# Soft-MoE chain on one core: more weight pieces held early, the second experts' first weights split earlier, one direct block instead of two

## The chip, the core and the metric

The kernel runs on one core of one Trainium2 chip. A core has a matrix engine (TensorE, PE in the profile, with its weight loads shown apart as PEld), three engines for elementwise work (VectorE = DVE, ScalarE = ACT, GpSimd = POOL) and SyncE (SP), which issues the transfers between HBM and the core's memory here. The metric is the device time of one execution in microseconds, the median of several. A smaller number is better.

## The reference

Three steps follow one another: causal attention with decay, a soft mixture of experts over slots, and a dense mixture of experts. Cut to what is computed:

```python
# attention: batch 4, heads 8, S = 576, D = 64
scores = q @ k.T / 8 + (cum_i - cum_j), causal     # cum: running sum of log(clip(f))
x = softmax(scores) @ v                            # -> x: 2304 tokens x 512

# soft MoE: 8 experts, 4 slots each, F = 1024
logits = x @ phi                                   # 2304 x 32
slot_in = softmax(logits, axis=tokens).T @ x       # 32 x 512
slot_out[e] = relu(slot_in[e] @ w1[e]) @ w2[e]     # 4 x 512 per expert
x = softmax(logits, axis=slots) @ slot_out         # 2304 x 512

# dense MoE: 4 experts, F = 1024, every token
p = domain_probs / (sum + 1e-9)
out = sum_e p[:, e] * (relu(x @ m1[e]) @ m2[e])
```

Below, w1 and w2 are the weights of the eight slot experts, and m1 and m2 those of the four dense experts.

## The kernel before

**Stages.** (a) Attention, pair of heads by pair of heads, up to about 212 us. (b) Its end, with the last softmax over the slots (212 to 222 us; the code from L540 to L645). (c) The eight slot experts (222 to 257 us): per expert `layer1` (32 matmuls, ReLU on ACT into `hr`), `turn` (two transposes of `hr`, a copy on DVE into `ht`) and `layer2` (16 matmuls, summed in `so_ps`). The last expert's second layer, `layer2_last`, is done in two halves of columns, and DVE adds each half to `orow0` and `orow1`. (d) A transition (257 to 265 us): the combine weights are transposed (`c4_tr`, copied by `c4_hi` on ACT into `c4t`), `g_make` multiplies the slots' outputs with m1 of dense expert 0 (so the first dense layer costs 32 rows of slots and not 2304 tokens), `g_spread` lays that out as `gs`. (e) The four dense experts, nine blocks of 256 tokens each, 36 blocks (265 to 673 us).

**A block of stage (e).** `pieces` (8 matmuls, `c4t` times `gs`) writes the hidden layer of a block into the PSUM tiles `two0` and `two1`, four matmuls for each. ACT and DVE take the ReLU out as two rounded parts, a hi part and a lo part (`q`, `a`, `s` in the rows). The second layer, hidden times m2, is done with operands of the type fp32r as hi times hi, hi times lo and lo times hi. A **direct** block (L1043 in the rows, `d`) does it with 96 matmuls of 128x256. A **Strassen** block (L1023, `R`, `P`, `Q`) has seven products of 12 matmuls, 84 in all, and DVE must make sums of hidden pieces for it (`S1` to `S4`, L893), POOL their lo parts (L901). In both kinds DVE takes the results out of PSUM, scaled by p, into `acc` (`take`, L1004 and L1006). There are four PSUM banks for results, used in turn: a new one cannot be begun before DVE has taken out the one that held the bank.

**Weights of stage (e).** m2 of an expert is a 512x512 grid of four parts, B00, B10, B01, B11. Each needs a hi part (`w_hi`, a cast, `wh_B` in the rows) and a lo part (`w_lo`, source minus hi, L722, `wl_B`). Strassen products need B00, B10, B11 and four sums of parts, T1 to T4, made by POOL (`w_sum`, L703) and split the same way (`wh_T`, `wl_T`). For dense expert 0, m2 arrives last of all early weights, B's are split in the transition and in block 0, and T's in blocks 0 and 1 (table `PRE0`). Blocks 0 and 1 are direct (`ND = 2`), the others Strassen.

**Weights' way in.** SP streams pieces of 512 KB in the order of `stream`: w1, w2 of the slot experts, then m1, m2 of the dense ones. In attention 4 pieces go to the tile `ring` and `NB = 29` to the pool `ringb`, one every third step; more go to freed memory (`raw`, `opd`, `post`, `post2`) and, during the slot experts, to freed ring slots (table `later`). The m2 of dense expert 0 goes into `ring` last, behind the code of slot expert 5.

**What sets the order.** From attention on, a scheduler orders what is not fixed. In a region `manual_schedule(engines=...)` the named engines run in the order in which the code stands. In the transition these are PE, ACT and DVE, in the blocks also POOL; an instruction on an engine runs only when all before it on that engine are done. `busy(n)` puts n 128x128 matmuls of the identity on PE whose result nobody reads; a matmul on f32 data shows as two in the rows.

Of the kernel before, what the change touches and what calls it, by code (L numbers as in the profile page):

```python
# [34 lines left out]
def soft_moe_kernel(tc, a, out):  # L35
# [10 lines left out]
    NB = 29  # L46
    ND = 2
    with ExitStack() as top:
# [871 lines left out]
        with tc.manual_schedule(engines={E.PE, E.Activation, E.DVE}):  # L920
            turn(E1 - 2)
            layer1(E1 - 1)
            layer2(E1 - 2)
            turn(E1 - 1)
            c4_tr(B, c4_bank(B))
            c4_tr(0, c4_bank(0))
            for h in range(2):
                act.copy(orow[h], so_ps[:, 256 * h:256 * h + 256])
            free += [0, 1, 2, 3]
            c4_hi(B)  # L930
            c4_hi(0)
            for h in range(2):
                layer2_last(h)
            c4_rep(2)
            c4_tr(1, c4_bank(1))
            c4_hi(1)
            c4_rep(3)
            t = bank(0, 0)[:, 0:128].rearrange("p (c s) -> p c s", c=DC)
            for c in range(DC):
                pe.matmul(t[:, c, :], lhsT=orow[c // 2][:, c % 2 * 128:c % 2 * 128 + 128], rhs=i4)  # L940
            dve.tensor_copy(so_t, t)
            c4_tr(2, c4_bank(2))
            c4_hi(2)
            w_hi(0, "B00", act, 0, 2)
            w_lo(0, "B00", pool, 0, 2)
            w_hi(0, "B00", act, 2, 4)
            gg = g_make(0, bank(0, 1)[:, 0:256])
            c4_tr(3, c4_bank(3))
            c4_hi(3)
            cq.close()  # L950
            attn.close()
            accp = top.enter_context(tc.tile_pool(name="accp", bufs=1))
            wsp.append(top.enter_context(tc.tile_pool(name="wspb", bufs=1)))
            top.enter_context(tc.tile_pool(name="skew", bufs=1)).tile([128, 24], F32, name="skew")
            hp = top.enter_context(tc.tile_pool(name="hp", bufs=1))
            ttp = top.enter_context(tc.tile_pool(name="ttp", bufs=1))
            free += [4, 5, 6, 7]
            for hf in range(2):
                g_spread(0, *gg, hf)
            pieces(0, 0)  # L960
            hi_d(0, 0, 0)
            lo_d(0, 0, 0)
            w_hi(0, "B10", act, 0, 2)
            w_lo(0, "B10", pool, 0, 2)
            hi_d(0, 0, 1)
            lo_d(0, 0, 1)
            pieces(0, 1)
            hi_d(0, 1, 0)
            lo_d(0, 1, 0)
            w_lo(0, "B00", dve, 2, 4)  # L970
            w_hi(0, "B10", act, 2, 4)
            w_lo(0, "B10", pool, 2, 4)
            hi_d(0, 1, 1)
            lo_d(0, 1, 1)
            w_hi(0, "B01", act, 0, 2)
            w_lo(0, "B01", pool, 0, 2)
            w_hi(0, "B01", act, 2, 4)
            w_lo(0, "B01", dve, 2, 4)
            w_hi(0, "B11", act, 0, 2)
            w_lo(0, "B11", pool, 0, 2)  # L980
            w_hi(0, "B11", act, 2, 4)
            w_lo(0, "B11", dve, 2, 4)
            dve.tensor_reduce(dps, dpr, axis=AX.X, op=ALU.add)
            dve.tensor_scalar(dps, dps, 1e-9, None, op0=ALU.add)
            dve.reciprocal(dps, dps)
            dve.tensor_tensor(dpn, dpr, dps[:, :, None].to_broadcast([128, 18, E2]), op=ALU.mult)
# [246 lines left out]
```

## Time and profile before

| | us |
|---|---|
| median of 3 runs (lowest to highest) | 675.01 (674.58 to 676.32) |
| the profiled execution | 675.4 |
| its span, first to last instruction | 673.6 |
| PE busy in the span | 657.5 (98%) |
| DVE, POOL, ACT busy | 494.5 (73%), 419.0 (62%), 341.8 (51%) |
| slot experts, 220 to 255 us: PE busy, share of the DMA engines | 33.9 of 35, 0.95 |
| blocks 0 and 1 of the dense experts (265.05 to 290.36) | 25.3 |
| mean granted clock of PE | 0.99 of full speed |

Times in rows are microseconds from the start of the span, and 1.8 us of the execution lie around the span. PE is busy almost throughout, so what changes the time is what PE has to do and where it waits. "Busy" of a matmul row reaches to its modelled end, so matmul rows overlap the next one's start; the pace is read from starts.

### The profile page before, as it was taken

Reading aid. Unit: us, or ns where it says so; the run is one execution under the profiler, and the core shown is the slowest. Engines: PE = TensorE matmul, PEld = TensorE weight load, DVE = VectorE, ACT = ScalarE, POOL = GpSimd, SP = SyncE. Lnnn points to the kernel's source line nnn. Section 1 sums busy time; section 2 is a strip of 40 time slices with the busy share of each in tenths; the row PEclk is TensorE's granted clock in tenths of the full one; section 3 lists DMA queues with packets and bytes.
Section 4 is the critical chain, followed back from the end, with each engine's and each line's share of the span. In section 5 each row is a group of like instructions: output and inputs, shape, how many; then the busy total and the mean of one; then the engine's idle time right before and its main releaser. Section 6 shows DMA issues by size and latency. Waiting matters only on the chain.

```text
span 673.6 us, 15304 instructions
## 1 busy us (share of the span) xinstructions
PE 657.5 (98%) x5642; PEld 580.3 (86%) x5642; DVE 494.5 (73%) x1358; ACT 341.8 (51%) x817; POOL 419.0 (62%) x392
## 2 busy tenths in 40 slices
PE   5999999999999998999999999999999999999997
PEld 3877777777777446999999999999999999999997
DVE  7888988988986103976778876778876778877774
ACT  4776767767763015543446443446543356543441
POOL 5677767767751046944589844589934589935442
PEclk7999999999999999999999999999999999999999
DMA  6678788733318894033000303000303000011111
GB/s 184 189 261 254 220 279 262 229 93 117 93 55 310 334 419 165 2 126 126 1 1 2 126 1 125 2 1 2 124 3 111 15 1 1 32 37 59 48 48 63
DMA packets 27138, 76.15 MB, mean 113 GB/s; under 512 B 3772, under 2 KB 4156, under 8 KB 27064
## 3 DMA queue, kind: packets, MB, share of 16 engines
q1 hardware_dynamic: 27064, 75.18, 32.5%
q8 instruction: 45, 0.74, 0.5%
q14 instruction: 29, 0.24, 0.1%
HBM read 70.31 MB, written 4.72 MB: 111 GB/s over the span
## 4 chain that ended last, share of the span: by engine, by line
PE 91%; DVE 3%; ACT 2%; issue 2%; SPq 1%; DMA 1%; POOL 0%; ACTq 0%; DVEq 0%
PE R L1023 27%; PE Q L1023 13%; PE P L1023 6%; PE avb L276 6%; PE pt L258 5%; PE two L835 5%; PE sc L228 3%; PE d L1043 3%; PE sc L212 3%; PE sc L227 3%; PE two L731 2%; PE pl L324 2%; PE pt L249 2%; PE ava L288 2%; PE so_ps L755 2%
## 5 line engine op out<-in xcount | busy, mean ns | idle before, releaser
L901 POOL TENSOR_TENSOR s<-S,s 128x512 fp32r<-128x512 f32 x136 | 174.9, 1320 | 134.7 <-ACT s L897 134.7
L897 ACT CAST s<-S 128x512 fp32r<-128x512 f32 x136 | 75.0, 619 | 85.9 <-DVE S L893 47.9
L202 ACT ACTIVATE p<-p,nm 128x256 f32<-128x256 f32 (+2 forms) x144 | 83.4, 580 | 37.7 <-DVE nm L198 36.9
L1023 PE MATMUL R<-wh_T,s 128*128 128x256 f32 x544 | 86.6, 281 | 0.7 <-DVE acc L1006 0.7
L1006 DVE SCALAR_TENSOR_TENSOR acc<-R,dpn,acc 128x256 f32<-128x256 f32 x115 | 55.4, 482 | 37.2 <-PE R L1023 34.2
L867 ACT ACTIVATE a<-two 128x256 f32<-128x256 f32 x68 | 26.1, 384 | 96.9 <-PE two L835 90.5
L1023 PEld LDWEIGHTS R<-wh_T,s 128*128 128x128 f32 x544 | 73.4, 188 | 1.4 <-ACT a L876 1.2
L198 DVE CUSTOM_DVE_ANT_0 p<-sc,maskb 128x256 f32<-128x256 f32 (+2 forms) x144 | 66.1, 488 | 3.3 <-PE sc L212 0.9
L893 DVE SCALAR_TENSOR_TENSOR S<-two,S 128x256 f32<-128x256 f32 x136 | 57.0, 419 | 3.4 <-POOL s L901 0.8
L893 DVE SCALAR_TENSOR_TENSOR S<-two,a 128x256 f32<-128x256 f32 x136 | 56.2, 413 | 0.0
L179 POOL TENSOR_TENSOR opd<-raw,opd 64x576 fp32r<-64x576 f32 x30 | 44.6, 1487 | 11.2 <-ACT opd L168 9.8
L258 PE MATMUL pt<-ident,p 128*128 128x128 f32 x288 | 47.3, 283 | 1.8 <-DVE ptb L255 0.8
L227 PE MATMUL sc<-opd 128*128 128x256 f32 (+3 forms) x128 | 47.1, 378 | 1.6 <-ACT opd L168 1.6
L190 POOL TENSOR_TENSOR opd<-raw,opd 64x576 fp32r<-64x576 f32 x31 | 44.1, 1424 | 6.7 <-DVE opd L170 5.7
L258 PEld LDWEIGHTS pt<-ident,p 128*128 128x128 f32 x288 | 31.3, 142 | 17.6 <-issue 13.1
L835 PE MATMUL two<-c4t,gs 128*128 128x256 f32 x288 | 46.1, 283 | 0.3 <-ACT gs L168 0.3
L883 DVE SCALAR_TENSOR_TENSOR q<-two,q 128x512 fp32r<-128x512 f32 x68 | 46.2, 679 | 0.0
L1023 PE MATMUL R<-wh_T,q 128*128 128x256 f32 x272 | 43.8, 283 | 0.0
L276 PE MATMUL avb<-ptb,v 128*64 128x192 f32 (+3 forms) x384 | 43.8, 347 | 0.0
L1023 PE MATMUL Q<-wh_B,s 128*128 128x256 f32 x272 | 43.2, 281 | 0.0
L1023 PE MATMUL Q<-wh_T,s 128*128 128x256 f32 x272 | 43.1, 280 | 0.0
L1023 PE MATMUL R<-wh_B,a 128*128 128x256 f32 x272 | 43.0, 280 | 0.0
(244 smaller groups left out, 1662.5 us busy)
## 6 DMA issues: line engine op xcount, KB each, us to landing
w<-in_w SPq DMA_DIRECT2D x50, 512.0 KB, 4.9
ring<-in_m SPq DMA_DIRECT2D x28, 512.0 KB, 6.2
raw<-in_k SPq DMA_DIRECT2D x64, 144.0 KB, 2.8
v<-in_v SPq DMA_DIRECT2D x16, 320.0 KB, 4.0
out<-acc SPq DMA_DIRECT2D x18, 256.0 KB, 2.0
...
```

What stands on the lines that cost most here:

```text
L198: dve.tensor_tensor_reduce(out=pt_in[j][:, k0:k0 + n], in0=sc, in1=maskb[:, m0:m0 + n], scale=-SCALE, scalar=nm, op0=ALU.add, op1=ALU.min, ...
L202: act.activation(p, p, AF.Exp, bias=nm, scale=-1.0, accum_out=sums)
L227: pe.matmul(o, lhsT=qa[hh][:, qs], rhs=ka[hh][:, 0:n], start=True, stop=False)
L258: pe.transpose(t[:, i, :], pt_in[j][:, 128 * i:128 * i + 128], ident)
L276: pe.matmul(t[64 * hh:64 * hh + 64, q0:q1], lhsT=v_raw[pr][:kk, i, 64 * hh:64 * hh + 64], rhs=ptb[2 * pr + hh][:kk, b0:b0 + q1 - q0], star ...
L835: pe.matmul(t[:, j, k], lhsT=gs[e][:, 128 * fc:128 * fc + 128], rhs=c4t[:, nb * BLK:nb * BLK + BLK])
L883: dve.scalar_tensor_tensor(o[:, 1], i, 0.0, f32(o[:, 0]), op0=ALU.max, op1=ALU.subtract)
L893: dve.scalar_tensor_tensor(sv[m, name][:, c], half[m, h][:, :, k, 128 * t:128 * t + 128], 0.0, other, op0=ALU.max, op1=op)
L897: act.copy(tile_of(m, name)[:, 0], sv[m, name])
L901: (eng or pool).tensor_tensor(o[:, 1], sv[m, name], f32(o[:, 0]), op=ALU.subtract)
L1006: dve.scalar_tensor_tensor(o, t, pcol, o, op0=ALU.mult, op1=ALU.add)
L1023: pe.matmul(t, lhsT=a[:, c, :], rhs=w[:, c, :], start=first and x == 0 and c == 0, stop=x == 2 and c == 3, skip_group_check=True)
```

## The change

It does seven things.

1. `NB` 29 to 33: `ringb` has four more slots, and four more pieces are loaded in attention (every third step, and now at steps 48 and 96 too).
2. In `stream`, m2 of dense expert 0 is moved forward, and goes to `ring` after slot expert 0, not after 5.
3. `busy(3)` is added at the end of attention, and four matmuls of the identity after `c4_tr(3)`.
4. The splits of B00, B10 and B01 are moved into slot experts 6 and 7: hi on ACT, lo on DVE, each 128x1024 in one instruction. B11 hi follows in the transition, B11 lo in block 0.
5. POOL's order is now written out from slot expert 6 on (before, from block 0 on). POOL makes T1, T2 before `g_spread`'s place, T3, T4 after it.
6. `ND` 2 to 1: only block 0 is direct. The table `PRE0` puts the sums and splits of the T's earlier, since block 1 needs them.
7. `dynamic_dma_scratch_size` is 256 and not the default, which moves the addresses of tiles on one side of the memory by 16128 bytes.

The rest of the diff is a change of indentation. Cut to its core:

```diff
-    NB = 29
-    ND = 2
+    NB = 33
+    ND = 1
...
+        at = NB + 19
+        stream = stream[:at] + stream[8 * E1 + 4:8 * E1 + 8] + stream[at:8 * E1 + 4] + stream[8 * E1 + 8:]
...
-                if pre and g >= GW and g % PS == PO:
+                if pre and g >= GW and (g % PS == PO or g % 48 == 0):
...
             dnat(B - 1)
+            busy(3)
...
-        later = {0: (ring, 4), 1: (ringb, 8), 2: (ringb, len(stream) - 44), 3: (ringb, 4), 5: (ring, 4)}
+        later = {0: (ringb, 8), 1: (ringb, 8)}
...
+            if e == 0:
+                raws[0] = load_ring()
             if e in later:
-                if later[e][0] is ring:
-                    raws[0] = load_ring()
-                else:
-                    load_w(*later[e])
+                load_w(*later[e])
...
-        with tc.manual_schedule(engines={E.PE, E.Activation, E.DVE}):
...
+        top.enter_context(tc.manual_schedule(engines={E.PE, E.Activation, E.DVE, E.Pool}))
+        free += [0, 1, 2, 3]
+        turn(E1 - 2)
+        w_hi(0, "B00", act)
+        w_hi(0, "B10", act)
+        w_lo(0, "B00", dve)
+        layer1(E1 - 1)
+        layer2(E1 - 2)
+        w_hi(0, "B01", act)
+        turn(E1 - 1)
+        w_lo(0, "B10", dve)
+        w_lo(0, "B01", dve)
+        c4_tr(B, c4_bank(B))
...
         c4_tr(3, c4_bank(3))
         c4_hi(3)
+        for _ in range(4):
+            pe.matmul(bank(1, 1)[:, 0:128], lhsT=ident, rhs=ident)
...
+        for name in ("T1", "T2"):
+            for c0 in (0, 2):
+                w_sum(0, name, c0, c0 + 2)
         for hf in range(2):
             g_spread(0, *gg, hf)
         pieces(0, 0)
         hi_d(0, 0, 0)
         lo_d(0, 0, 0)
...
+        w_lo(0, "B11", dve)
...
-                (1, 0): [("hi", "T1", "a", 0, 4), ("lo", "T2", "d", 0, 4)],
-                (1, 1): [("lo", "T1", "p", 0, 4), ("hi", "T3", "a", 0, 4)],
...
+        PRE0 = {(0, 0): [("sum", "T3", 0, 2), ("sum", "T3", 2, 4), ("hi", "T1", "a", 0, 4)],
+                (0, 1): [("lo", "T1", "d", 0, 2)],
...
-    nc = bacc.Bacc("TRN2", target_bir_lowering=False, num_devices=1)
+    nc = bacc.Bacc("TRN2", target_bir_lowering=False, num_devices=1, dynamic_dma_scratch_size=256)
```

What the edits do to the order on the engines, at three places. In these rows a name ends in a number of its own, `ring_28`, `ring_44` are the tile with m2, `wh_0_B00` and `wl_0_B00` the hi and lo part of B00 of dense expert 0, and `two0`, `two1` the PSUM tiles.

DVE around slot experts 6 and 7, before:

```order
L746 COPY ht_7_3593<-two0_3240 128x8x4
L767 TENSOR_TENSOR orow0_3556<-orow0_3556,two1_3241 128x256
L767 TENSOR_TENSOR orow1_3557<-orow1_3557,two1_3241 128x256
L941 COPY so_t_3520<-two0_3240 128x128
L911 CAST gh_0_3676<-two0_3240 128x256
L912 TENSOR_TENSOR gl_0_3677<-two0_3240,gh_0_3676 128x256
L170 CAST gs_0_3680<-two1_3241 128x512
```

DVE at the same place, now:

```order
L749 COPY ht_6_3569<-two0_3252 128x8x4
L725 TENSOR_TENSOR wl_0_B00_3573<-ring_44_3328,wh_0_B00_3572 128x1024
L749 COPY ht_7_3610<-two0_3252 128x8x4
L725 TENSOR_TENSOR wl_0_B10_3576<-ring_44_3328,wh_0_B10_3575 128x1024
L725 TENSOR_TENSOR wl_0_B01_3606<-ring_44_3328,wh_0_B01_3605 128x1024
L770 TENSOR_TENSOR orow0_3563<-orow0_3563,two1_3253 128x256
L770 TENSOR_TENSOR orow1_3564<-orow1_3564,two1_3253 128x256
L949 COPY so_t_3527<-two0_3252 128x128
```

Three subtractions of 128x1024 now stand between the copies `ht_6`, `ht_7` and the two additions to `orow`, which PE needs for the slots' outputs.

DVE from the last lo part of block 0's hidden layer to the first results of block 0 (`acc0`, `acc1`), before; `q1_1`, `q2_1` are the hidden layer of block 1:

```order
L846 SCALAR_TENSOR_TENSOR q2_0_3727<-two1_3241,q2_0_3727 128x512
L722 TENSOR_TENSOR wl_0_B01_3742<-ring_28_3505,wh_0_B01_3741 128x512
L722 TENSOR_TENSOR wl_0_B11_3748<-ring_28_3505,wh_0_B11_3747 128x512
L983 TENSOR_REDUCE dps_3524<-dpr_3523 128x18
L846 SCALAR_TENSOR_TENSOR q1_1_3831<-two0_3240,q1_1_3831 128x512
L984 TENSOR_SCALAR dps_3524<-dps_3524 128x18
L985 RECIPROCAL dps_3524<-dps_3524 128x18
L986 TENSOR_TENSOR dpn_3521<-dpr_3523,dps_3524 128x72
L846 SCALAR_TENSOR_TENSOR q2_1_3834<-two0_3240,q2_1_3834 128x512
L1004 TENSOR_SCALAR acc0_3758<-d_0_0_0_3778,dpn_3521 128x256
L1004 TENSOR_SCALAR acc1_3759<-d_0_0_1_3779,dpn_3521 128x256
```

DVE at the same place, now, behind the last lo part of block 0's hidden layer, `w_lo` of B11 (128x1024) and the first of the small ones; `S1_1` to `S4_1` and `a11_1` are operands of the Strassen products of block 1:

```order
L983 TENSOR_SCALAR dps_3531<-dps_3531 128x18
L984 RECIPROCAL dps_3531<-dps_3531 128x18
L985 TENSOR_TENSOR dpn_3528<-dpr_3530,dps_3531 128x72
L725 TENSOR_TENSOR wl_0_T1_3805<-T1_0_3726,wh_0_T1_3804 128x512
L895 SCALAR_TENSOR_TENSOR S1_1_3846<-two0_3252,a21_1_0_3825 128x256
L895 SCALAR_TENSOR_TENSOR S2_1_3848<-two0_3252,S1_1_3846 128x256
L725 TENSOR_TENSOR wl_0_T1_3805<-T1_0_3726,wh_0_T1_3804 128x512
L885 SCALAR_TENSOR_TENSOR a11_1_3827<-two0_3252,a11_1_3827 128x256
L895 SCALAR_TENSOR_TENSOR S3_1_3875<-two0_3252,a21_1_0_3825 128x256
L895 SCALAR_TENSOR_TENSOR S4_1_3877<-two0_3252,S2_1_3848 128x256
L725 TENSOR_TENSOR wl_0_T2_3853<-T2_0_3729,wh_0_T2_3852 128x512
L1003 TENSOR_SCALAR acc0_3766<-d_0_0_0_3784,dpn_3528 128x256
```

Between the last lo part of block 0's hidden layer and the first result there were two weight splits, four small ones (`dps`, `dpn`) and two lo parts; now there are four weight splits (B11, twice T1, T2), the four small ones, and five operands of block 1.

POOL after the last combine weights (`c4_3`), before:

```order
L703 TENSOR_TENSOR T1_0_3796<-ring_28_3505 128x512
L722 TENSOR_TENSOR wl_0_B00_3656<-ring_28_3505,wh_0_B00_3655 128x512
L703 TENSOR_TENSOR T1_0_3796<-ring_28_3505 128x512
L722 TENSOR_TENSOR wl_0_B10_3724<-ring_28_3505,wh_0_B10_3723 128x512 x2
L722 TENSOR_TENSOR wl_0_B01_3742<-ring_28_3505,wh_0_B01_3741 128x512
L703 TENSOR_TENSOR ring_28_3505<-ring_28_3505 128x2x256
L722 TENSOR_TENSOR wl_0_B11_3748<-ring_28_3505,wh_0_B11_3747 128x512
L703 TENSOR_TENSOR ring_28_3505<-ring_28_3505 128x2x256
L703 TENSOR_TENSOR T2_0_3877<-T1_0_3796,ring_28_3505 128x512 x2
L703 TENSOR_TENSOR ring_28_3505<-ring_28_3505,T2_0_3877 128x2x256 x2
```

POOL at the same place, now:

```order
L706 TENSOR_TENSOR T1_0_3726<-ring_44_3328 128x512 x2
L706 TENSOR_TENSOR T2_0_3729<-T1_0_3726,ring_44_3328 128x512 x2
L706 TENSOR_TENSOR ring_44_3328<-ring_44_3328 128x2x256 x2
L706 TENSOR_TENSOR ring_44_3328<-ring_44_3328,T2_0_3729 128x2x256 x2
L725 TENSOR_TENSOR wl_0_T2_3853<-T2_0_3729,wh_0_T2_3852 128x512
L725 TENSOR_TENSOR wl_0_T3_3902<-ring_44_3328,wh_0_T3_3901 128x512
L903 TENSOR_TENSOR s0_1_3937<-S2_1_3848,s0_1_3937 128x512
L903 TENSOR_TENSOR s0_1_3937<-S1_1_3846,s0_1_3937 128x512
```

POOL's splits of B's are gone, and the eight sums run one behind the other, followed by half of the lo parts of T2 and T3 and then the lo parts of block 1's operands (`s0_1`), which in the kernel before only block 2 has.

## Rows read from the trace of the kernel before

**Rows 1.** The page's part 1: busy time, share of the span, instructions of each engine.
```profile
PE 657.5 (98%) x5642; PEld 580.3 (86%) x5642; DVE 494.5 (73%) x1358; ACT 341.8 (51%) x817; POOL 419.0 (62%) x392
```

**Rows 2.** What PE waited for: us in total, times, longest.
```profile
PE two L765 <- DVE orow L767: 0.6, 1, 0.6
...
PE two L820 <- DVE gl L912: 0.4, 1, 0.4
...
PE sa_e L614 <- DVE dnn L397: 0.4, 1, 0.4
...
PE d L1043 <- DVE wl_B L722: 0.2, 1, 0.2
```

**Rows 3.** Windows: us, each engine's busy time (instructions), granted clock, DMA share, GB/s.
```profile
220.00:255.00 35.00, 33.91 (x430) 15.69 (x426) 2.70 (x12) 4.83 (x13) 9.98 (x29) 1.00 0.95 378
...
268.00:290.00 22.00, 21.77 (x186) 21.57 (x185) 19.87 (x31) 12.49 (x23) 20.12 (x13) 1.00 0.08 27
```

**Rows 4.** PE's timeline: start, us, line, tiles, shapes, count [idle before].
```profile
216.55 1.16 PE L540 MATMUL busy<-ident 128*128 128x128 f32 x8
...
217.64 0.47 PE L395 MATMUL dn<-ident,dt_e 32*128 32x32 f32 x5
...
256.34 1.07 PE L765 MATMUL two<-w,ht 128*32 128x256 f32 x16 [0.61 <-DVE orow L767]
...
265.05 0.39 PE L1043 MATMUL d<-wh_B,q 128*128 128x256 f32 x1 [0.17 <-ACT q L842]
...
290.36 0.63 PE L1023 MATMUL R<-wh_B,a 128*128 128x256 f32 x4
```

**Rows 5.** DVE's timeline, slot expert 7 to block 1, same columns.
```profile
254.21 0.19 DVE L746 COPY ht<-two 128x32 f32<-128x32 f32 x1 [3.87 <-PE ct L673]
...
255.86 0.42 DVE L767 TENSOR_TENSOR orow<-orow,two 128x256 f32<-128x256 f32 x1 [1.46 <-PE two L765]
...
269.20 0.68 DVE L846 SCALAR_TENSOR_TENSOR q<-two,q 128x512 fp32r<-128x512 f32 x1
...
272.58 0.22 DVE L983 TENSOR_REDUCE dps<-dpr 128x18 f32<-128x72 f32 x1
...
274.18 0.97 DVE L986 TENSOR_TENSOR dpn<-dpr,dps 128x72 f32<-128x72 f32 x1
...
279.19 1.97 DVE L722 TENSOR_TENSOR wl_T<-T,wh_T 128x1024 fp32r<-128x1024 f32 x1
...
281.87 2.65 DVE L722 TENSOR_TENSOR wl_T<-ring,wh_T 128x1024 fp32r<-128x1024 f32 x1
```

**Rows 6.** POOL's timeline, transition to block 1.
```profile
261.87 1.29 POOL L703 TENSOR_TENSOR T<-ring 128x512 f32<-128x512 f32 x1 [2.61 <-issue]
...
277.52 2.56 POOL L703 TENSOR_TENSOR ring<-ring,T 128x512 f32<-128x512 f32 x2
...
280.04 3.40 POOL L722 TENSOR_TENSOR wl_T<-T,wh_T 128x1024 fp32r<-128x1024 f32 x1
...
283.38 3.40 POOL L722 TENSOR_TENSOR wl_T<-ring,wh_T 128x1024 fp32r<-128x1024 f32 x1
```

**Rows 7.** The weight splits on DVE by source: duration in ns, min/median/max.
```profile
L722 DVE TENSOR_TENSOR wl_T<-ring,wh_T x10: 678/682/2648, 281.9 to 581.5; 128x512 fp32r<-128x512 f32 x9, 128x1024 fp32r<-128x1024 f32 x1
```

**Rows 8.** The chain that ended last, in order of time: one product of 12 matmuls.
```profile
293.81 1.41 PE R L1023 x12
```

**Rows 9.** Groups by line and shape: busy us, mean ns of one, idle before.
```profile
L716 ACT CAST wh_B<-ring 128x1024 fp32r<-128x1024 f32 x9 | 9.4, 1049 | 0.0
...
L893 DVE SCALAR_TENSOR_TENSOR S<-two,a 128x256 f32<-128x256 f32 x136 | 56.2, 413 | 0.0
...
L883 DVE SCALAR_TENSOR_TENSOR a<-two,a 128x256 fp32r<-128x256 f32 x68 | 28.1, 414 | 0.0
...
L1004 DVE TENSOR_SCALAR acc<-d,dpn 128x256 f32<-128x256 f32 x8 | 3.5, 474 | 1.6 <-PE d L1043 1.6
```

**Rows 10.** SP's timeline: the four transfers of m2 of dense expert 0.
```profile
247.78 3.05 SPq L71 DMA_DIRECT2D ring<-in_m  x4
```

More of the change, by code (lines that the diff above doesn't have):

```diff
@@ L839, in hi_d @@
                 ss[m, k] = (hp.tile([128, 2, 4, 256], F32R, tag="q2", bufs=2, name=f"q2_{m}") if k else
-                            hp.tile([128, 2, 4, 256], F32R, tag=f"s{m % 2}", name=f"q1_{m}"))
+                            hp.tile([128, 2, 4, 256], F32R, tag="s1", name=f"q1_{m}"))
             o = ss[m, k][:, 0, 2 * h:2 * h + 2][:, js]
@@ L918, in c4_bank @@
             return ops.tile([128, DM], F32, tag="o", name=f"ct_{b}")
-        with tc.manual_schedule(engines={E.PE, E.Activation, E.DVE}):
[L921 to L986, printed above, removed]
@@ new lines, in soft_moe_kernel @@
+        top.enter_context(tc.manual_schedule(engines={E.PE, E.Activation, E.DVE, E.Pool}))
[11 more added lines that the diff above has]
+        c4_tr(B, c4_bank(B))
+        c4_tr(0, c4_bank(0))
+        for h in range(2):
+            act.copy(orow[h], so_ps[:, 256 * h:256 * h + 256])
@@ new lines, in soft_moe_kernel @@
+        c4_hi(B)
+        c4_hi(0)
+        for h in range(2):
+            layer2_last(h)
+        c4_rep(2)
+        c4_tr(1, c4_bank(1))
+        c4_hi(1)
+        c4_rep(3)
+        t = bank(0, 0)[:, 0:128].rearrange("p (c s) -> p c s", c=DC)
+        for c in range(DC):
+            pe.matmul(t[:, c, :], lhsT=orow[c // 2][:, c % 2 * 128:c % 2 * 128 + 128], rhs=i4)
+        dve.tensor_copy(so_t, t)
+        c4_tr(2, c4_bank(2))
+        c4_hi(2)
+        w_hi(0, "B11", act)
+        gg = g_make(0, bank(0, 1)[:, 0:256])
@@ new lines, in soft_moe_kernel @@
+        c4_tr(3, c4_bank(3))
+        c4_hi(3)
+        for _ in range(4):
+            pe.matmul(bank(1, 1)[:, 0:128], lhsT=ident, rhs=ident)
+        cq.close()
+        attn.close()
+        accp = top.enter_context(tc.tile_pool(name="accp", bufs=1))
+        wsp.append(top.enter_context(tc.tile_pool(name="wspb", bufs=1)))
+        top.enter_context(tc.tile_pool(name="skew", bufs=1)).tile([128, 24], F32, name="skew")
+        hp = top.enter_context(tc.tile_pool(name="hp", bufs=1))
+        ttp = top.enter_context(tc.tile_pool(name="ttp", bufs=1))
@@ new lines, in soft_moe_kernel @@
+        free += [4, 5, 6, 7]
+        for name in ("T1", "T2"):
+            for c0 in (0, 2):
+                w_sum(0, name, c0, c0 + 2)
+        for hf in range(2):
+            g_spread(0, *gg, hf)
+        pieces(0, 0)
+        hi_d(0, 0, 0)
+        lo_d(0, 0, 0)
+        hi_d(0, 0, 1)
+        lo_d(0, 0, 1)
+        pieces(0, 1)
+        hi_d(0, 1, 0)
+        lo_d(0, 1, 0)
+        hi_d(0, 1, 1)
+        lo_d(0, 1, 1)
+        w_lo(0, "B11", dve)
+        dve.tensor_reduce(dps, dpr, axis=AX.X, op=ALU.add)
@@ L987, in soft_moe_kernel @@
+        dve.tensor_scalar(dps, dps, 1e-9, None, op0=ALU.add)
+        dve.reciprocal(dps, dps)
+        dve.tensor_tensor(dpn, dpr, dps[:, :, None].to_broadcast([128, 18, E2]), op=ALU.mult)
         acc = [accp.tile([128, DM], F32, name=f"acc{i}") for i in range(18)]
```

168 lines of the change are left out of this document (83 added, 85 removed), and 7 rows, old and new, of the table PRE0.

## The prediction

> **What bounds the kernel now.** I read the busy shares first: PE is busy for 657.5 of 673.6 us [rows 1], so the time is what PE has to do, plus its few waits. The PE's own waits come next, and only four of them lie near the change: 0.6 us for `orow`, 0.4 for `gl`, 0.4 for `dnn` and 0.2 for a weight's lo part [rows 2]. The windows say that neither stage which the change touches starves PE. The slot experts keep PE busy for 33.91 of 35 us though the DMA engines are 0.95 busy, and blocks 0 and 1 keep it busy for 21.77 of 22 us. In that second window, however, DVE is busy for 19.87 and POOL for 20.12 of 22 us [rows 3]. That is what the reader should keep in mind: there is no room on DVE and POOL in just the stretch into which the change puts more of their work. PE's granted clock is 1.00 in both windows, so the clock gives nothing back there.
>
> The numbers below are made against the profiled execution, 675.4 us with a span of 673.6; the median of the runs is 675.0, so a sum of +x means 675.0 + x for the median.
>
> **Transfers (edits 1, 2, 7): 0.** PE is busy throughout attention, and the four more transfers there are issued by SP, which does no arithmetic. During the slot experts four pieces fewer are asked for, but PE had only 1.1 us of idle time there, little of it for weights. m2 of dense expert 0, which SP issued at 247.78 before [rows 10], now goes into the queue about 25 us sooner. It must: its first cast now runs at about 250. At 378 GB/s a piece of 0.52 MB takes 1.4 us, and some 13 pieces stand before its end from 222 on, so it is there at about 240. With 10 us to spare I take 0, with 0 to +0.5 as bounds. The moved addresses have no row; I take 0.
>
> **`busy(3)` (edit 3): +0.3.** A filler matmul on f32 data makes two rows; eight rows take from 216.55 to 217.64, 0.136 us each [rows 4]. Six are 0.8 us. They stand where PE waited 0.4 us for `dnn` [rows 2], so 0.4 is left, less about 0.1 for the overlap of a row with the next. Range 0.2 to 0.4.
>
> **Four fillers after `c4_tr(3)`: +0.55.** Eight rows of 0.136 are 1.1 us, in place of the 0.4 us for which PE waited for `gl` [rows 2]; 0.1 overlaps. If `gl` comes later by more than that, they are free, but the next paragraph moves PE and DVE alike, so I keep 0.45 to 0.65.
>
> **Splits in the slot experts (edit 4): +1.0.** On ACT the three casts of 1.05 us [rows 9] fit between the ReLUs of experts 6 and 7. On DVE, idle there, lo B00 fits before the copy `ht_7`. Lo B10 and lo B01 do not: they stand behind `ht_7` and ahead of the `orow` additions. `ht_7` ends at 254.40 [rows 5]. A 128x512 split takes 0.68 when nothing disturbs it [rows 7], so one of 128x1024 takes about 1.2 to 1.3, and two end at about 256.8, where the first `orow` addition used to begin at 255.86 [rows 5]. PE's second half of `layer2_last`, which began at 256.34 after its wait [rows 4], waits for that addition: +1.0. Bounds: 0.5 if the copy `ht_7` is released 0.4 earlier (it waited for a `ct` transposition behind the one it needs), 1.7 if POOL's operations on `c4_2` come between.
>
> **One direct block less, no lo waits (edits 4 and 6): -2.3.** From the first direct matmul to the first of block 2 there are 25.31 us [rows 4]. Twelve matmuls take 1.41 [rows 8], 0.117 each. The new pair is 96 + 84 matmuls of the second layer and 16 of `pieces`, 196 x 0.117 = 23.0 us, if PE waits for nothing. That is 1.4 for twelve matmuls fewer and 0.9 for waits on lo parts of B's, which are now made before.
>
> **DVE's new queue in blocks 0 and 1 (edits 4, 5, 6): +3.3.** This is the term that decides. I count from block 0's first matmul.
>
> PE needs 12.2 us for block 0 (96 matmuls and 8 of `pieces`, of 0.117). Block 1's first product then needs the bank of block 0's first result, so `take` must be past. DVE ends the last lo part of block 0's hidden layer at +4.0 (before at 269.88 [rows 5], +4.8, with a weight split of its own between). Behind it stand, in order: lo B11 1.2; the four small ones, which take 1.9 from 272.58 to 275.15 less one lo part of 0.68 [rows 5]; half of lo T1 0.68; S1, S2 0.83; half of lo T1 0.68; `a_lo` 0.41; S3, S4 0.83; half of lo T2 0.68; the take 0.47 [rows 7, 9]. That is 7.7, less 0.8 since each starts some 0.07 before the end of the one ahead. To this come the waits for POOL, worked out in the next paragraph, 1.8. The take is done at 4.0 + 7.7 - 0.8 + 1.8 = 12.7: PE waits 0.5 there. Then DVE has a second take 0.47, a lo part 0.68 (block 2's `pieces` wait for it), S1 to S4 1.65, `a_lo` 0.41, two takes 0.95, a lo part 0.68, half of lo T3 0.68 with 0.7 of waiting, and the take of block 1's first product 0.48: 6.0 net of overlaps, so 18.7. PE's third product adds into that very bank, and undisturbed it is due after 104 + 24 + 4 = 132 matmuls, at 15.4. So PE is late by 3.3 in all, in three or four waits of 0.3 to 1.5 each. Behind it the chain is shorter than PE's work, and I expect nothing more.
>
> The waits for POOL come from a pair of rows. A lo T of 128x1024 on DVE started at 279.19 while POOL's sums ran until 280.08, and took 1.97, where two of 0.68 would be 1.3. POOL's split, begun at 280.04, took 3.40, where two of 1.28 are 2.56; DVE's next, begun at 281.87 in that split, took 2.65 and ended 1.1 after it [rows 5, 6]. So a subtraction on DVE with both inputs in SBUF and one on POOL seem to run one after the other, never together. In block 0 POOL has eight sums and two halves of lo parts of 1.28 each in a row, from about the end of `g_make` until +10. Each two-input operation on DVE meets one that is half through on the mean, 0.6: lo B11, one half of T1, and 0.6 more on the small ones than in their rows: 1.8. Bounds: without any such exclusion the term is +0.3, and with a full POOL operation of waiting each time +5.
>
> The Trainium skill says the same in "SBUF — State Buffer", section "Who interferes with whom": a DVE instruction with two SBUF inputs contends with a POOL instruction that reads SBUF, and the one that comes second blocks fully. By that rule the term is the +3.3; if the rows had another cause it would be +0.3. The trace agrees with the rule [rows 5, 6].
>
> **Sum.** 0 + 0.3 + 0.55 + 1.0 - 2.3 + 3.3 = +2.9: 678.3 for the profiled execution, 677.9 for the median.
>
> **Rivals.** What a measurement of this kernel can tell from no change is about 0.3%, 2.0 us, so "same" is 673.0 to 677.0.
>
> *DVE keeps up (not slower).* If the rows of 1.97 and 2.65 us owe their length to something other than the exclusion, DVE has 4.0 + 7.7 - 0.8 = 10.9 at the first take, before the 12.2 at which PE asks for it. That is the point which decides: 1.3 us of waits for POOL. The last term becomes +0.3 or less, the sum 0.3 + 0.55 + 1.0 - 2.3 + 0.3 = -0.15, 674.9; the favourable bounds (0.2, 0.45, 0.5, 0) give -1.15, 673.9. With half of the waits it is near 676. For it: DVE waits are worked out, not seen, and POOL's order could leave DVE first. Against it: three rows fit the exclusion to 0.1 us.
>
> *Faster.* Were the fillers and the splits in front of `orow` to cost nothing as well, -2.3 would stand alone, 672.7. Against it: a filler is PE time, and there is only 0.8 us of waiting for both [rows 2].
>
> *The queue runs on into block 2.* DVE also has takes of seven products in block 1, lo T3, lo T4 (twice 0.68) and block 2's operands. If it is not level by the end of block 1, `pieces` of block 2 and its first products wait too, +1.5 to +2: 679.5 to 680. For it: DVE was busy for 19.87 of 22 us [rows 3].
>
> *Early splits wait for m2.* If m2 came at 253 and not at 240, lo B00 would hold `ht_7` and with it PE, us for us: +3 at most, on top. SP's order and the 10 us to spare speak against it; I count it to the case before.
>
> **How the numbers follow.** Forecast, 677.0 to 679.3 about 677.9: 0.52. DVE keeps up, 673.9 to 677.0: 0.30. Faster than 673.0: 0.08. Slower still, about 680: 0.10. The predicted time is the first case's. The range 674.3 to 680.0 leaves out the fast case, the lowest part of the second and the upper half of the last, 0.2 in all. Faster by over 0.3%: 0.08. Within: 0.30. Slower: 0.62.
>
> **What would show it.** In the profile of the changed kernel: PE's wait before the second half of `layer2_last` near 1.6 us, for DVE's `orow` (against: 0.6); no wait for a lo part of a B; two rows more of fillers where 0.4 us of waiting stood; from the first direct matmul to block 2's first product 26.4 us (against: 23 to 23.5), with PE waiting for DVE's `acc` and `q` in block 1's first products; DVE busy almost without a gap there, its splits longer than 0.68 where POOL works. I am wrong if the two blocks take under 24.5 us, or if a stretch outside 216 to 293 us changes by over 0.5 us.

## The result and the profile after

The changed kernel took **679.85 us** (median of 4; 677.63 to 681.69), the kernel before beside it 674.87. The ratio is 1.0063 with a 95% interval of 1.0036 to 1.0090: slower by 5.0 us by the two medians and by 4.3 by the ratio, where 677.9 with a range of 674.3 to 680.0 was forecast. (The ratio, here and below, is not simply the quotient of the two medians.) The profiled execution is the longest one, 681.7 us with a span of 679.9. The busy row stands beside [rows 1]:

```profile
PE 661.6 (97%) x5644; PEld 582.9 (86%) x5644; DVE 501.2 (74%) x1374; ACT 343.8 (51%) x819; POOL 415.3 (61%) x391
```

PE's share fell from 98 to 97%. Its waits (us in total, times, longest) answer to [rows 2]:

```profile
PE R L1022 <- DVE acc L1003: 2.0, 2, 1.4
...
PE two L768 <- DVE orow L770: 1.2, 1, 1.2
...
PE P L1022 <- DVE q L885: 0.4, 1, 0.4
```

The waits for `gl`, for `dnn` and for the lo part of a B are gone. The wait for `orow` has doubled, and new are 2.0 us for the takes of results out of PSUM (L1003) and 0.4 for a lo part of block 1. PE's timeline shows the places (compare [rows 4]):

```profile
223.19 3.61 PE L734 MATMUL two<-ring,si_t 128*32 128x256 f32 x32
...
259.33 1.07 PE L768 MATMUL two<-w,ht 128*32 128x256 f32 x16 [1.21 <-DVE orow L770]
...
264.56 1.06 PE L957 MATMUL two<-ident 128*128 128x128 f32 x8
...
265.37 0.37 PE L822 MATMUL two<-gh,sel 128*128 128x256 f32 x1
...
268.26 0.39 PE L1042 MATMUL d<-wh_B,q 128*128 128x256 f32 x1 [0.18 <-ACT q L844]
...
281.26 0.71 PE L1022 MATMUL R<-wh_B,a 128*128 128x256 f32 x4 [0.56 <-DVE acc L1003]
...
285.33 0.50 PE L1022 MATMUL P<-wh_B,q 128*128 128x256 f32 x2 [0.36 <-DVE q L885]
...
287.26 0.72 PE L1022 MATMUL R<-wh_T,s 128*128 128x256 f32 x4 [1.44 <-DVE acc L1003]
...
289.29 1.05 PE L1022 MATMUL Q<-wh_T,s 128*128 128x256 f32 x4
...
296.41 0.63 PE L1022 MATMUL R<-wh_B,a 128*128 128x256 f32 x4
```

From the first direct matmul (268.26) to block 2 (296.41) there are 28.15 us, where it was 25.31. The row at 289.29 shows something that no row of before has there: four matmuls that took 0.63 take 1.05. The row at 223.19 is of the same kind: 32 matmuls in 3.61 us, where the same 32 of the next expert take 1.93. The windows of one us (columns as in [rows 3], the granted clock third from the end) tell why:

```profile
222.00:223.00 1.00, 1.00 (x9) 0.88 (x8) 0.34 (x2) 0.00 (x0) 0.24 (x1) 1.00 0.00 0
...
225.00:226.00 1.00, 1.00 (x16) 0.58 (x12) 0.00 (x0) 0.00 (x0) 0.00 (x0) 0.50 1.01 414
...
286.00:287.00 1.00, 0.00 (x0) 0.00 (x0) 1.00 (x2) 1.00 (x4) 1.00 (x2) 1.00 0.00 0
...
289.00:290.00 1.00, 1.00 (x7) 1.00 (x6) 1.00 (x3) 0.00 (x0) 0.09 (x1) 0.50 0.00 0
...
292.00:293.00 1.00, 1.00 (x11) 1.00 (x11) 0.63 (x2) 0.81 (x3) 0.00 (x0) 1.00 0.28 57
```

PE was granted 1.00 of its clock (2.4 GHz), then 0.50 (1.2 GHz) from 223.2 to 226.6 and again from 288.1 to 291.5, then 1.00. Neither stretch was in the prediction.

DVE's rows stand against [rows 5]:

```profile
256.25 0.19 DVE L749 COPY ht<-two 128x32 f32<-128x32 f32 x1 [1.94 <-PE two L746]
...
256.39 2.56 DVE L725 TENSOR_TENSOR wl_B<-ring,wh_B 128x1024 fp32r<-128x1024 f32 x2
...
272.16 1.93 DVE L725 TENSOR_TENSOR wl_B<-ring,wh_B 128x1024 fp32r<-128x1024 f32 x1
...
274.26 1.02 DVE L983 TENSOR_SCALAR dps<-dps 128x18 f32<-128x18 f32 x1
...
275.61 0.98 DVE L985 TENSOR_TENSOR dpn<-dpr,dps 128x72 f32<-128x72 f32 x1
...
276.51 0.68 DVE L725 TENSOR_TENSOR wl_T<-T,wh_T 128x512 fp32r<-128x512 f32 x1
...
277.90 1.22 DVE L725 TENSOR_TENSOR wl_T<-T,wh_T 128x512 fp32r<-128x512 f32 x1
...
280.65 0.86 DVE L1003 TENSOR_SCALAR acc<-d,dpn 128x256 f32<-128x256 f32 x2
...
285.19 1.53 DVE L725 TENSOR_TENSOR wl_T<-ring,wh_T 128x512 fp32r<-128x512 f32 x1
...
286.64 0.47 DVE L1003 TENSOR_SCALAR acc<-R,dpn 128x256 f32<-128x256 f32 x1
```

DVE has hardly a gap from 271.5 to 291.6. Its first take begins at 280.65, 12.4 us after the first direct matmul, and the take at 286.64, for which the third product waits, at 18.4. A split of 128x512 takes 0.68 (276.51), 1.22 or 1.53.

### The profile page after: what moved, and what is told of

Read it like the earlier page. It is cut to its first block, busy times and chain, and to the rows that moved or that the text cites. A ratio compares the mean times of both kernels' runs of the same rounds, so it can differ in the third digit from the quotient of the medians.

```text
span 679.9 us, 15328 instructions
## 1 busy us (share of the span) xinstructions
PE 661.6 (97%) x5644; PEld 582.9 (86%) x5644; DVE 501.2 (74%) x1374; ACT 343.8 (51%) x819; POOL 415.3 (61%) x391
## 4 chain that ended last, share of the span: by engine, by line
PE 89%; DVE 5%; issue 2%; ACT 2%; SPq 1%; DMA 1%; POOL 0%; ACTq 0%; DVEq 0%
PE R L1022 27%; PE Q L1022 14%; PE P L1022 6%; PE avb L278 6%; PE pt L260 5%; PE two L837 5%; PE sc L230 3%; PE sc L229 3%; PE sc L214 3%; PE two L734 2%; PE pl L326 2%; PE pt L251 2%; PE ava L290 2%; PE so_ps L758 2%; PE two L909 1%
## 5 line engine op out<-in xcount | busy, mean ns | idle before, releaser
L903 POOL TENSOR_TENSOR s<-S,s 128x512 fp32r<-128x512 f32 x140 | 180.2, 1320 | 143.9 <-ACT s L899 143.9
L899 ACT CAST s<-S 128x512 fp32r<-128x512 f32 x140 | 77.3, 619 | 92.2 <-DVE S L895 61.6
L1022 PE MATMUL R<-wh_T,s 128*128 128x256 f32 x560 | 89.6, 282 | 2.1 <-DVE acc L1003 1.4
L1022 PEld LDWEIGHTS R<-wh_T,s 128*128 128x128 f32 x560 | 76.0, 189 | 2.9 <-ACT q L878 1.6
L895 DVE SCALAR_TENSOR_TENSOR S<-two,S 128x256 f32<-128x256 f32 x140 | 58.6, 419 | 3.4 <-POOL s L903 0.7
L895 DVE SCALAR_TENSOR_TENSOR S<-two,a 128x256 f32<-128x256 f32 x140 | 57.8, 413 | 0.0
L885 DVE SCALAR_TENSOR_TENSOR q<-two,q 128x512 fp32r<-128x512 f32 x70 | 47.6, 679 | 0.0
L1022 PE MATMUL R<-wh_B,a 128*128 128x256 f32 x280 | 44.6, 281 | 0.6 <-DVE acc L1003 0.6
L1022 PE MATMUL P<-wh_B,q 128*128 128x256 f32 x280 | 44.5, 280 | 0.4 <-DVE q L885 0.4
L1022 PE MATMUL Q<-wh_T,s 128*128 128x256 f32 x280 | 44.7, 282 | 0.0
```

The costliest lines, as they stand in the source:

```text
L885: dve.scalar_tensor_tensor(o[:, 1], i, 0.0, f32(o[:, 0]), op0=ALU.max, op1=ALU.subtract)
L895: dve.scalar_tensor_tensor(sv[m, name][:, c], half[m, h][:, :, k, 128 * t:128 * t + 128], 0.0, other, op0=ALU.max, op1=op)
L899: act.copy(tile_of(m, name)[:, 0], sv[m, name])
L903: (eng or pool).tensor_tensor(o[:, 1], sv[m, name], f32(o[:, 0]), op=ALU.subtract)
L1022: pe.matmul(t, lhsT=a[:, c, :], rhs=w[:, c, :], start=first and x == 0 and c == 0, stop=x == 2 and c == 3, skip_group_check=True)
```

## The experiments

The first four kernels were timed beside one another on one chip, the next four on a second, the last two on the first again; the kernel before, beside them, took 675.65, 675.65 and 675.72 us. Where a time is told by stage it comes from PE's timeline of that kernel's profiled execution: first direct matmul to block 2's first product is "blocks 0 and 1". The start of attention's last group `avb`, at 209.2 to 210.8 us in profiles of kernels that are the same up to there, shows how far executions differ by themselves.

**The changed kernel again.** No edit.

> The changed kernel once more, unaltered. In its profiled execution PE's granted clock stood at 0.50 in two short stretches, 223.7 to 226.6 us and 288 to 291.5 us, in which the matmuls took 3.3 us longer than at 1.00. Theory 'two costs': the waits and the added work give about +2.9 us in every execution, and the low clock 0 to 3.3 us on top, in some executions and not in others. Then the executions spread from about 677.6 to 681.7, and those with the lower mean clock (0.987) are the longer ones, those with 0.992 the shorter ones. Rival 'always': the low clock belongs to the change's order; then every execution has both stretches, and the times lie within 1 us of each other.

Measured: 679.76 us (678.35 to 682.06, ratio 1.0067, 1.0050 to 1.0084). In its profile the stretch at half clock in block 1 is there again, that at 224 us is not (PE's timeline, then windows).

```profile
267.46 0.39 PE L1042 MATMUL d<-wh_B,q 128*128 128x256 f32 x1 [0.18 <-ACT q L844]
...
295.60 0.64 PE L1022 MATMUL R<-wh_B,a 128*128 128x256 f32 x4
```

```profile
224.00:225.00 1.00, 0.92 (x20) 0.71 (x24) 0.00 (x0) 0.00 (x0) 0.21 (x1) 1.00 0.37 98
...
288.00:289.00 1.00, 1.00 (x6) 1.00 (x6) 0.98 (x2) 0.00 (x0) 0.29 (x1) 0.50 0.00 0
```

Blocks 0 and 1: 28.14 us. Both theories were half right. The one in block 1 goes with the change: it stands in all four profiles that have its three waits (this kernel twice, and the next two), though perhaps not in every execution, since one of the six had a mean clock of 0.995 where this profile has 0.990. The one at 224 us comes and goes: 1.7 us, from the two rows of 32 matmuls. The mean clock of the executions goes the same way, if loosely: the longest of the six (682.06) had 0.987, the shortest (678.35) 0.995. The kernel before has such executions too, 678.3 and 680.1 us at 0.987 and 0.986 beside most at 674.5 to 676.5 and 0.992.

**Without `busy(3)`.**

```diff
             dnat(B - 1)
-            busy(3)
```

> The changed kernel without the three matmuls of the identity at the end of attention. By the sum: -0.4 us, and PE waits 0.4 for the copy before L614 again. If these matmuls bring on the low clock at 223.7 us (they are the only thing PE does otherwise before it), that stretch is gone too: the row of the first 32 matmuls of slot expert 0 takes 1.9 to 2.0 us and not 3.6, and the median falls by 1 to 2 us. If not, the median falls by 0.4 and the stretch at half clock comes as often as before.

Measured: 678.15 us (677.79 to 681.65, ratio 1.0048, 1.0029 to 1.0067). From the last `avb` of attention to slot expert 0 there are 12.87 us, as in the kernel before, and 13.27 with the three matmuls: they cost 0.40. The larger step of the median, 1.6, is not explained by that, and the intervals overlap. Of the 1.95 us between the two profiled executions (680.55 and 678.60), 1.6 lie ahead of `avb` (210.80 and 209.18), where the two kernels are the same. The stretch in block 1 stays. One of the six executions had a mean clock of 0.987 and 681.65 us, which speaks against these matmuls as the cause of the low clock at 224 us, though no trace of that execution shows where it was low.

**Without the four fillers.**

```diff
-        for _ in range(4):
-            pe.matmul(bank(1, 1)[:, 0:128], lhsT=ident, rhs=ident)
```

> The changed kernel without the four matmuls of the identity behind the last transposition of combine weights. By the sum: -0.2 to -0.5 us, with a wait of about 0.4 for the second part of g in their place. The stretch at half clock in block 1 (288 to 291.5 us) stays if it is brought on by PE's waits in block 1; if these fillers have to do with it, it goes or comes earlier.

Measured: 679.94 us (677.21 to 680.90, ratio 1.0059, 1.0041 to 1.0077), no difference that the times can tell. The rows can: from the second half of `layer2_last` to `g_spread` 5.82 us and not 6.04, so the fillers cost 0.22; the wait of 0.42 for `gl` is back, and block 1 is as it was, half clock included: it needs no fillers.

**Without POOL's sums T3 and T4** (products that use them get unsummed weights).

```diff
-            (eng or pool).tensor_tensor(o[:, c], x[:, c], y[:, c], ...)
+            if e or name not in ("T3", "T4"):
+                (eng or pool).tensor_tensor(o[:, c], x[:, c], y[:, c], ...)
```

> The changed kernel with POOL's sums T3 and T4 of dense expert 0 left out (the products that use them get unsummed weights; nothing else differs, DVE's list is the same). Theory 'exclusion': DVE's splits and the small operations in block 0 were long because POOL ran sums at the same time. Then lo B11 takes about 1.2 and not 1.93 us, the small ones 0.2 to 0.3 and not 1.02 and 0.98, the first take comes 2 us earlier, PE's first wait in block 1 (0.56) is gone and the one before the third product falls from 1.44 to under 0.5; blocks 0 and 1 fall by 1 to 2 us, plus what the half clock cost there if that is brought on by these waits. Rival 'lengths of their own': the DVE rows keep their lengths and blocks 0 and 1 take the same time.

Measured: 676.87 us (675.98 to 677.43, ratio 1.0011, 0.9995 to 1.0027). DVE's list is the same, and its rows shrink as the theory said (timeline of DVE, then of PE):

```profile
270.62 1.22 DVE L726 TENSOR_TENSOR wl_B<-ring,wh_B 128x1024 fp32r<-128x1024 f32 x1
...
272.01 0.18 DVE L984 TENSOR_SCALAR dps<-dps 128x18 f32<-128x18 f32 x1
...
282.05 1.54 DVE L726 TENSOR_TENSOR wl_T<-ring,wh_T 128x512 fp32r<-128x512 f32 x1
```

```profile
266.73 0.39 PE L1043 MATMUL d<-wh_B,q 128*128 128x256 f32 x1 [0.18 <-ACT q L845]
...
279.00 0.63 PE L1023 MATMUL R<-wh_B,a 128*128 128x256 f32 x4
...
284.13 0.72 PE L1023 MATMUL R<-wh_T,s 128*128 128x256 f32 x4 [1.44 <-DVE acc L1004]
...
291.94 0.63 PE L1023 MATMUL R<-wh_B,a 128*128 128x256 f32 x4
```

Lo B11 takes 1.22 and not 1.93, the second small operation 0.18 and not 1.02. PE does not wait at block 1's first product (279.00). The wait before the third product stays at 1.44: the split of T3 in front of the take it waits for took 1.54 again; in both kernels POOL works on the lo parts `s` there, and these were left in. Blocks 0 and 1 take 25.21 us, 2.9 less than with the sums, and PE's clock stays at 1.00. So POOL's work is what makes DVE's rows long, and the one wait of 1.44 alone did not bring on the low clock here.

**The small operations earlier.**

```diff
         dve.tensor_copy(so_t, t)
+        dve.tensor_reduce(dps, dpr, axis=AX.X, op=ALU.add)
...
         w_lo(0, "B11", dve)
-        dve.tensor_reduce(dps, dpr, axis=AX.X, op=ALU.add)
...
```

> The changed kernel with the four small DVE operations on the domain weights (dps, dpn) moved from block 0 to right behind the copy of so_t, where DVE waits for PE for about 2 us. Theory 'exclusion and queue': they took 2.5 us in block 0, so DVE is ahead by that there: PE's wait at block 1's first product (0.56) is gone, that for the lo part of A12 (0.36) too, that before the third product stays at 0.4 to 1.4 us, since the split of T3 next to it still meets POOL. Blocks 0 and 1 take 25.2 us and not 28.1 (as without POOL's sums, 25.2), with no stretch at half clock; the median falls by 2.5 to 3. Rival: the half clock comes from the single long wait before the third product; then it stays, and blocks 0 and 1 fall by 1 us only.

Measured: 676.70 us (676.34 to 677.48, ratio 1.0010, 0.9996 to 1.0024). DVE's timeline, then PE's:

```profile
270.23 1.94 DVE L725 TENSOR_TENSOR wl_B<-ring,wh_B 128x1024 fp32r<-128x1024 f32 x1
...
272.08 1.79 DVE L725 TENSOR_TENSOR wl_T<-T,wh_T 128x512 fp32r<-128x512 f32 x1
```

```profile
266.33 0.39 PE L1042 MATMUL d<-wh_B,q 128*128 128x256 f32 x1 [0.18 <-ACT q L844]
...
278.61 0.63 PE L1022 MATMUL R<-wh_B,a 128*128 128x256 f32 x4
...
291.64 0.64 PE L1022 MATMUL R<-wh_B,a 128*128 128x256 f32 x4
```

Blocks 0 and 1: 25.31 us, what they were before the change. The first and second wait are gone, the third (1.42) stays, the clock stays at 1.00. Four small operations, 0.9 us together in their new place, had cost 2.8 us of the kernel, 1.3 of them by the clock. The splits behind them, 1.94 and 1.79 us, still meet POOL's sums.

**Two direct blocks.**

```diff
-    ND = 1
+    ND = 2
...
-            ... tag="s1", name=f"q1_{m}"))
+            ... tag=f"s{m % 2}", name=f"q1_{m}"))
```

> The changed kernel with two direct blocks again, not one; all else as changed. By the sum: 12 matmuls more (+1.4), but block 1 needs no sums of hidden pieces and no split of T's in block 0, so PE does not wait for DVE there, and the clock stays at 1.00. Blocks 0 and 1 take 24.4 to 24.9 us and not 28.1, the median falls by 3 to 4 us, to about that of the kernel before plus 1. If DVE's queue is not the cause of the lost time, blocks 0 and 1 take 28.1 + 1.4 us.

Measured: 676.72 us (675.33 to 678.01, ratio 1.0000, 0.9985 to 1.0015). PE's timeline:

```profile
266.38 0.39 PE L1042 MATMUL d<-wh_B,q 128*128 128x256 f32 x1 [0.17 <-ACT q L844]
...
279.39 0.36 PE L1042 MATMUL d<-wh_B,q 128*128 128x256 f32 x1 [0.59 <-DVE acc L1003]
...
291.64 0.63 PE L1022 MATMUL R<-wh_B,a 128*128 128x256 f32 x4
```

Blocks 0 and 1: 25.26 us, 0.4 more than expected, with the one wait of 0.59 for a take. So they take less with 12 matmuls more: the Strassen form of block 1 saved 1.4 us of matmuls and cost 4.3.

**Fillers where PE waits.**

```diff
+            if m == 1 and s == 2:
+                tq = ops.tile([128, DM], F32, tag="o", name=f"Q_{m}")
+                chain[m, "Q"] = [tq[:, 0:256], True]
+                for _ in range(5):
+                    pe.matmul(tq[:, 256:384], lhsT=ident, rhs=ident)
```

> The changed kernel with five matmuls of the identity ahead of block 1's third product, where PE waits 1.44 us for DVE: 10 passes, 1.0 to 1.4 us, so the third product starts at most 0.1 later. Theory 'waits bring the low clock': PE then waits only 0.56 + 0.36 in block 1 and 0.1 to 0.4 at the third product, the granted clock stays at 1.00 from there on, and blocks 0 and 1 take 26.5 us and not 28.1, the median falls by 1.6. Rival: the low clock comes from something else that block 1 does (Strassen products with splits made just before); then it stays, and blocks 0 and 1 take 28.1 to 28.3.

Measured: 678.71 us (677.74 to 681.06, ratio 1.0043, 1.0028 to 1.0059). PE's timeline, then a window from the place where the clock had been 0.50:

```profile
266.71 0.39 PE L1047 MATMUL d<-wh_B,q 128*128 128x256 f32 x1 [0.18 <-ACT q L844]
...
284.12 1.28 PE L1018 MATMUL Q<-ident 128*128 128x128 f32 x10
...
285.71 0.72 PE L1027 MATMUL R<-wh_T,s 128*128 128x256 f32 x4 [0.31 <-DVE acc L1003]
...
293.53 0.63 PE L1027 MATMUL R<-wh_B,a 128*128 128x256 f32 x4
```

```profile
287.00:288.00 1.00, 1.00 (x11) 1.00 (x10) 1.00 (x1) 0.00 (x0) 0.55 (x1) 1.00 0.00 0
```

The fillers take the wait's place, the third product starts no later (19.0 us after the first direct matmul, as in the changed kernel), and the clock stays at 1.00. From there to block 2 there are 7.82 us, where it was 9.15: the half clock costs 1.33. Blocks 0 and 1 take 26.82 us, 0.3 more than expected. The ratio falls by 0.0024, or 1.6 us, as expected, though the intervals overlap. So PE's waits bring on the low clock here. In these profiles it took the long one and the two ahead of it together, since neither the long one alone nor the other two with a filled third did it.

**Reordered.** The small operations and lo B01 behind the copy of `so_t`; the second half of lo T3 behind the take of block 1's first product; no `busy(3)`, no fillers.

```diff
-        w_lo(0, "B01", dve)
...
         dve.tensor_copy(so_t, t)
+        w_lo(0, "B01", dve)
+        dve.tensor_reduce(dps, dpr, axis=AX.X, op=ALU.add)
...
-                (1, 0): [("lo", "T3", "d", 2, 4)], (1, 2): ...
+                (1, 1): [("lo", "T3", "d", 2, 4)], (1, 2): ...
```

> The changed kernel with what the experiments so far point to: the four small operations and lo B01 moved behind the copy of so_t, the second half of lo T3 behind the take of block 1's first product, and both groups of identity matmuls left out. By the sum: no busy(3) -0.4, orow 0.6 to 1.2 us earlier, no fillers -0.2, blocks 0 and 1 at 23.0 to 24 us and not 28.1, no stretch at half clock: 3.5 to 4 us below the changed kernel's fastest executions, so 673.0 to 674.0 on a chip where the kernel before takes 675.0. Rival: waits move to POOL (lo B01 and the small operations meet its combine weights or its first sums); then 674.5 to 675.5.

Measured: 676.07 us (673.84 to 679.93, ratio 0.9998, 0.9980 to 1.0016). The miss has a place: the wait for `orow` fell only to 0.61, what it was before the change, and blocks 0 and 1 took 25.54 where 23.0 to 24 was expected. DVE itself waits 0.65 for PE ahead of that addition now, so the 0.61 is no queue of DVE but the way from PE to DVE and back, the addition of 0.42 included. Lo T4 stands ahead of two takes, and took 1.67 us beside POOL (DVE's timeline, then PE's):

```profile
284.28 1.67 DVE L724 TENSOR_TENSOR wl_T<-ring,wh_T 128x512 fp32r<-128x512 f32 x1
...
285.88 0.47 DVE L1000 TENSOR_SCALAR acc<-R,dpn 128x256 f32<-128x256 f32 x1
```

```profile
286.50 0.72 PE L1019 MATMUL R<-wh_T,s 128*128 128x256 f32 x4 [0.84 <-DVE acc L1000]
```

**Lo T4 later.**

```diff
-                ... (1, 2): [("lo", "T4", "d", 0, 2)], (1, 3): [("lo", "T4", "d", 2, 4)]}
+                ... (1, 4): [("lo", "T4", "d", 0, 2)], (1, 5): [("lo", "T4", "d", 2, 4)]}
```

> e10_reordered with both halves of lo T4 two products later (they stood ahead of the takes of block 1's third and fourth product and met POOL's lo parts: 1.67 us in place of 0.68). Theory 'exclusion and queue': PE's waits of 0.84 and 0.31 us in block 1 go, blocks 0 and 1 take 24.3 to 24.6 us and not 25.5; 1 us below e10_reordered, 0.7 to 1.0 below the kernel before. Rival: the two splits then stand in front of what block 2 needs; blocks 0 and 1 shorten, block 2 lengthens by the same.

Measured: 675.71 us beside 675.72 (ratio 0.9996, 0.9982 to 1.0010). Blocks 0 and 1 take 24.58 us, as expected, and block 2 takes the 10.81 us of the kernel before. The waits of 0.84 and 0.31 are gone, and a new one of 0.44, for the second half of lo T4, stands in block 1's last product. The gain of 0.7 us on the kernel before is too small to show in the times.

**B11 early too.**

```diff
         w_hi(0, "B01", act)
+        w_hi(0, "B11", act)
...
-        for h in range(2):
-            layer2_last(h)
+        layer2_last(0)
+        w_lo(0, "B01", dve)
+        layer2_last(1)
...
         dve.tensor_copy(so_t, t)
-        w_lo(0, "B01", dve)
+        w_lo(0, "B11", dve)
```

> e12 with one more step: lo B01 between the two orow additions, where DVE waits 1.26 us for PE, and B11 split before g_make too (hi behind hi B01 on ACT, lo behind the copy of so_t on DVE), so DVE has no weight split of B's left in block 0. Theory 'exclusion and queue': lo B11 took 2.15 us there; without it no wait for DVE is left in block 1, blocks 0 and 1 take 23.0 to 23.4 us, and the sum is -1.9 to -2.3 against the kernel before, less 0.1 to 0.3 if lo B01 holds up the second orow addition: 0.9970 to 0.9975. Rival: the hi cast of B11 holds up the copies of orow and the combine weights on ACT, PE waits there by 0.5 to 0.7, and little is left.

Measured: 673.84 us (672.51 to 676.35), the kernel before beside it 675.72: ratio 0.9971, 0.9956 to 0.9986, as expected. It is faster than the kernel before and than the changed one. DVE's timeline, then PE's:

```profile
273.51 0.86 DVE L1000 TENSOR_SCALAR acc<-d,dpn 128x256 f32<-128x256 f32 x2
...
278.99 0.49 DVE L1000 TENSOR_SCALAR acc<-R,dpn 128x256 f32<-128x256 f32 x1 [0.64 <-PE R L1019]
```

```profile
264.62 0.39 PE L1039 MATMUL d<-wh_B,q 128*128 128x256 f32 x1 [0.18 <-ACT q L843]
...
287.52 0.50 PE L1019 MATMUL R<-wl_T,q 128*128 128x256 f32 x2 [0.36 <-DVE wl_T L724]
```

DVE's first take begins 8.9 us after the first direct matmul, and from 278.99 on DVE waits for PE again. Blocks 0 and 1 take 23.71 us (block 2 begins at 288.33), with one wait left, 0.36 for the second half of lo T4. That is 0.3 above the longest time expected, and 1.6 below the kernel before; the stages from `avb` to block 0 take what they took there.

## Why the prediction was right or wrong

The direction and the mechanism were right and the time lay in the range, but the forecast was 1 to 2 us short, and the term that it lacked is the clock. That the time lies in the range is in part luck: it is 0.15 us below the upper end, and the prediction put the range's upper part there for a queue that runs on into block 2, which did not happen. Against the kernel before, in the profile of the changed kernel's second run:

| step | forecast | measured | from |
|---|---|---|---|
| transfers | 0 | 0 | no wait of PE for a weight is new |
| `busy(3)` | +0.3 | +0.4 | 13.28 us and not 12.87, `avb` to slot expert 0 |
| splits ahead of `orow` | +1.0 | +0.6 | 3.26 and not 2.66, `ct` to second half |
| four fillers | +0.55 | +0.23 | 6.04 and not 5.81, to `g_spread` |
| matmuls and lo waits | -2.3 | -1.95 | 23.35 (the last experiment less its wait) and not 25.31 |
| DVE's queue | +3.3 | +3.5 | 26.82 (fillers where PE waits) less 23.35 |
| half clock in block 1 | not there | +1.3 | 9.15 and not 7.82 |
| sum | +2.9 | +4.1 | |

The medians beside that profile, 679.76 and 675.65, differ by 4.1 too. The errors of the other terms, +0.1, -0.4, -0.3, +0.35 and +0.2, cancel, so the sum is short by the clock term alone; that too is luck. The first pair of medians differs by 5.0. The changed kernel's first profile has the other stretch at half clock (1.7 us) and its second has not; whether the 0.9 is that, four executions cannot tell.

*Transfers.* Right. SP issued m2 at 226.86, and no cast waited for it; the four pieces in attention show nowhere beyond the 1.6 us by which the start of `avb` differs among profiles.

*`orow`.* The mechanism was right: the two splits run back to back behind `ht_7` (256.39, 2.56 us), and PE waits for the addition behind them. The size was the lower bound that was named, since the copy `ht_7` was released 0.4 earlier. The step that failed is the choice between the two.

*Fillers.* Mis-sized: eight rows took 0.81 us there (264.56 to 265.37), 0.10 each and not 0.136. A price from one place [rows 4] did not hold at the other.

*DVE's queue.* Right, term by term: the first take was done 12.9 us after the first direct matmul (forecast 12.7), the third product began at 19.0 (18.7), and PE waited 0.56, 0.36 and 1.44 (forecast 0.3 to 1.5 each). These idle times, 2.4 in all, are counted from a matmul's modelled end; by starts the third product came 3.6 late, at 19.0 and not 15.4. That POOL's work lengthens DVE's rows, read from [rows 5, 6], was shown by leaving out POOL's sums. That one engine waits for the whole instruction of the other fits the rows (1.02 us for 128x18 elements) but was not tried by itself. The rule of the Trainium skill in "SBUF — State Buffer", section "Who interferes with whom", agrees: lo B11 took 1.93 us beside POOL's sums and 1.22 without them. That section says that a tensor_scalar can contend as well, when its operands meet conditions; here the one on 128x18 (L983) took 1.02 us beside POOL's sums and 0.18 without them. The small operations had been priced from rows of before that already held part of that.

*The clock.* The prediction said that the clock gives nothing back, and did not ask what new waits would take from it. Three waits stood before the fall to 0.50, and the kernels with fewer, shorter or filled waits did not have it. That a stretch of waits has a second price was the missing term. The mean clocks of the executions carry this beyond single profiles. Every profile has about 10 us at 0.50 near its start, which alone makes a mean of 0.992; one later stretch of 3.4 us makes 0.990, two make 0.987. On the first chip 11 of 18 executions of the three kernels with the three waits had 0.990 or less, none of 11 without POOL's sums, and 3 of 17 of the kernel before. The rival that runs on into block 2 did not happen: block 2 takes 10.8 us as before.

*What stays open.* What brings on the half clock at 224 us in some executions; only one profile shows it. Why the median without `busy(3)` fell by 1.6 us, where its rows show 0.4. Why blocks 0 and 1 without waits take 23.35 us and not the 22.9 of 196 matmuls. The moved addresses were not tried alone; the last experiment has them too and is faster all the same.
